# Second layer's weight conversion in a fused attention and two-layer kernel: in-place sums, four staging buffers, an earlier raw fetch

## The chip, the core and the metric

The kernel runs on one core of a Trainium2 chip. Its time is the device time of one execution in microseconds. Five engines work side by side, each with a queue of its own that it takes in order: TensorE (PE), VectorE (DVE), ScalarE (ACT), GpSimd (POOL) and SyncE (SP), which here issues all transfers between HBM and on-chip memory.

## What is computed

Attention through a small set of packed queries, then two feed-forward layers over 4608 tokens of width 512. The weights come as 64-bit floats.

```
p_packed = softmax(p @ k.T * scale) @ v          # 32 packed rows a head
x  = softmax(q @ p_packed.T * scale) @ p_packed   # 8 batches x 576 tokens, 8 heads x 64
h  = x @ w_in                                     # 512 -> 2048
x1 = (max(h, 0) + alpha * min(h, 0)) @ w_out      # 2048 -> 512
g  = x1 @ w_gate;  v = x1 @ w_val                 # 512 -> 1536
out = (g * sigmoid(g) * v) @ w_out2               # 1536 -> 512
```

## The kernel before

Matrix products are made of three products each, of a value rounded to a shorter format (hi) and its remainder (lo): hi by hi, hi by lo, lo by hi.

**First layer.** 256 iterations, each a group of 288 tokens by 128 hidden units. In iteration `it`, PE runs `h_unit(it)` (six matmuls into one of two PSUM banks "h"), then `o_unit(it - 3)` (twelve matmuls into four accumulators; `LAG1` is 3). Between them stands a chain over three engines: ACT makes `m` from h (L1003), DVE makes `g` from h and m (L1006) and so frees the bank, ACT rounds g to `hi` (L1014), POOL takes the difference `lo` (L1016). Attention of the later batches runs in between, by a table of half iterations: iteration `it` has the half `2*it`, ahead of `h_unit`, and `2*it + 1`, behind it. From iteration 224 on, the second layer's first tokens are made ready too: `split_x` rounds sums of x into ring tiles (L1120 on ACT, L1121 on DVE). Two of the eight ring tiles, tag D, take over the two buffers that the weight conversion works in.

**Conversion of the second layer's weights.** From half iteration 84 on. The 1536 hidden units are 12 blocks of 128 (`f`, 0 to 11). A block needs three raw pieces, of w_gate, w_val and w_out2, each 128 x 512 64-bit numbers. `widen` turns a piece into 32-bit floats by integer steps: SP fetches it into `raw` (L217); ACT takes the high words into a half tile `g` or `v` (L222); five steps follow on DVE (L224, L228, L237, L246, L254) and an addition on POOL (L265). From w_gate's and w_val's halves b11, b21, b12, b22 come four differences t1 to t4 (L927, POOL), since the second layer uses seven products in place of eight. Each of seven 256-column operands is split into hi (L933, ACT) and lo (L934, POOL) in a staging buffer and stored to HBM (L935, SP). w_out2's piece goes through `g` again and is split in 512 columns (L944, L945, L947). The tile `cva` with the lower number holds `raw`, `g` and `v`; the other one `t` and two staging buffers `st`, used in turn.

**What sets the order.** The conversion is a generator that yields "v" ahead of a DVE step and "p" ahead of a POOL or split step. `more_weights2` takes at most two steps in each half iteration, one "v" among them, and none of those in halves that attention keeps busy. The source order of all this is the wish only: the program is built by a scheduler that follows a simulated time line and lets instructions of one engine pass each other where their data allow it. After that the order on each engine is fixed, and the profile has exactly that order.

**Second layer.** Six groups of 768 tokens by 12 blocks, 72 steps of `gv_step`: seven products of six matmuls each (`product`), with ACT's p (L1204) and s (L1209) behind the first and the third, and the products with w_out2 of earlier steps between. The third product of a step (A12) reads x in the second ring tile and, in its second half, in the first tile of tag D; the fourth and fifth need the second tile of tag D. PE's order is the same in both programs.

## Time and profile before

| | us |
|---|---|
| median of 3 runs (1701.35 to 1706.72) | 1701.75 |
| the profiled execution | 1702.91 |
| its span, first to last instruction | 1701.1 |
| PE busy | 1609.9 (95%) |
| DVE, ACT, POOL busy | 868.2, 683.0, 708.8 |
| first layer's last matmul, second layer's first | 859.3, 859.5 |

The busy time of PE is not its peak: matmuls overlap. A row of the timeline gives start, length, engine, source line, operation and in brackets the idle time of the engine before it with what ended it. The view of waits adds such idle times up by the line that waited and the line or transfer waited for. The granted clock is 1.00 for 2.4 GHz and 0.5 for 1.2 GHz.

### The profile page before, as it was taken

To read this page: it belongs to the slowest core of one execution; us is meant where nothing else is said; L and a number is where in the kernel's file an instruction comes from. 1 tells how busy PE (TensorE), PEld (TensorE's weight loads), DVE (VectorE), ACT (ScalarE), POOL (GpSimd) and SP (SyncE) were. 2 spreads that over 40 slices of the span, in tenths; PEclk is the share of its full clock that TensorE was granted. 3 is DMA by queue.
4 is the path that set the end of the run, shared out by engine and by line. 5 is a ranking of instruction groups with operands and counts; after the bars stand their busy time and mean duration, and the time that the engine had idled before them with its cause. 6 is when DMAs were issued, how large, how long until landed. Compare 5 with 4: busy or idle time off the path is not lost.

```text
span 1701.1 us, 28474 instructions
## 1 busy us (share of the span) xinstructions
PE 1609.9 (95%) x10708; PEld 1456.6 (86%) x10708; DVE 868.2 (51%) x1549; ACT 683.0 (40%) x1511; POOL 708.8 (42%) x752
## 2 busy tenths in 40 slices
PE   5688899999999989999899999999999999999997
PEld 3467798988888888889899999999999999999997
DVE  6999757565756656565533443443443343244222
ACT  5774645555544555454522232232232232123122
POOL 3556744565554654547622322322322222232222
PEclk7799999999999999999999999999999999999999
DMA  9433464635445362644573463465455456445442
GB/s 238 121 102 115 120 159 115 165 95 155 130 108 143 117 156 53 150 138 139 182 274 141 177 237 139 166 202 185 164 211 182 158 191 202 159 174 185 156 173 81
DMA packets 227369, 266.11 MB, mean 156 GB/s; under 512 B 130464, under 2 KB 189856, under 8 KB 227232
## 3 DMA queue, kind: packets, MB, share of 16 engines
q1 hardware_dynamic: 227232, 264.30, 49.2%
q8 instruction: 84, 1.38, 0.3%
q14 instruction: 53, 0.43, 0.1%
HBM read 214.70 MB, written 49.55 MB: 155 GB/s over the span
## 4 chain that ended last, share of the span: by engine, by line
issue 39%; PE 25%; POOL 17%; DMA 7%; DVE 6%; ACT 4%; SPq 1%; POOLq 0%; ACTq 0%; DVEq 0%
POOL pl L1247 8%; PE acc L1029 5%; PE acc L1030 5%; PE acc L1035 5%; POOL s L1227 4%; DMA wgvd<-cva 4%; PE h L305 3%; PE h L307 2%; PE h L306 2%; POOL lo L1016 1%; DMA cva<-in_moe_w_gate_dram 1%; POOL cva L934 1%; DVE g L1006 1%; PE ppw L564 1%; POOL cva L265 1%
## 5 line engine op out<-in xcount | busy, mean ns | idle before, releaser
L1016 POOL TENSOR_TENSOR lo<-g,hi 128x288 fp32r<-128x288 f32 x256 | 227.5, 890 | 240.6 <-ACT hi L1014 187.8
L1227 POOL TENSOR_TENSOR s<-s,u 128x384 f32<-128x384 f32 x72 | 73.0, 1014 | 489.9 <-ACT s L1221 489.9
L1006 DVE SCALAR_TENSOR_TENSOR g<-h,sg,m 128x288 f32<-128x288 f32 x256 | 130.3, 509 | 162.2 <-ACT m L1003 132.0
L1184 DVE TENSOR_TENSOR u<-yb,p 128x384 f32<-128x384 f32 x144 | 80.1, 556 | 255.6 <-PE yb L307 255.6
L1247 POOL TENSOR_TENSOR pl<-s,ph 128x384 fp32r<-128x384 f32 x144 | 145.5, 1032 | 106.4 <-ACT ph L1245 106.4
L305 PE MATMUL h<-a2h,ppw 128*128 128x288 f32 x512 | 163.2, 319 | 27.0 <-DVE g L1006 21.4
L1184 DVE TENSOR_TENSOR u<-vb,u 128x384 f32<-128x384 f32 x144 | 80.4, 558 | 197.3 <-PE vb L307 196.9
L1014 ACT ACTIVATE hi<-g 128x288 fp32r<-128x288 f32 x256 | 113.1, 442 | 155.5 <-DVE g L1006 149.1
L307 PE MATMUL o<-wp,ph 128*128 128x512 f32 x432 | 171.5, 397 | 0.0
L306 PE MATMUL o<-wp,ph 128*128 128x512 f32 x432 | 170.9, 396 | 0.0
L305 PE MATMUL o<-wp,pl 128*128 128x512 f32 x432 | 168.8, 391 | 0.9 <-POOL pl L1247 0.9
L1221 ACT ACTIVATE s<-p 128x384 f32<-128x384 f32 x72 | 37.9, 526 | 302.0 <-DVE p L1184 302.0
L307 PE MATMUL h<-a2l,ppw 128*128 128x288 f32 x512 | 153.0, 299 | 0.0
L306 PE MATMUL h<-a2h,ppw 128*128 128x288 f32 x512 | 152.5, 298 | 0.0
L305 PEld LDWEIGHTS h<-a2h,ppw 128*128 128x128 f32 x512 | 97.9, 191 | 62.4 <-DVE g L1006 33.0
L305 PE MATMUL yb<-ring,gv 128*128 128x384 f32 x432 | 146.0, 338 | 0.2
L307 PE MATMUL yb<-ring,gv 128*128 128x384 f32 x432 | 144.4, 334 | 0.0
L306 PE MATMUL yb<-ring,gv 128*128 128x384 f32 x432 | 144.4, 334 | 0.0
L1003 ACT ACTIVATE m<-h,sal 128x288 f32<-128x288 f32 x256 | 125.6, 492 | 41.5 <-PE h L307 40.6
L1245 ACT ACTIVATE ph<-s 128x384 fp32r<-128x384 f32 x144 | 69.8, 519 | 121.3 <-DVE s L1225 121.3
L307 PEld LDWEIGHTS h<-a2l,ppw 128*128 128x128 f32 x512 | 98.0, 191 | 0.8 <-issue 0.8
L306 PEld LDWEIGHTS h<-a2h,ppw 128*128 128x128 f32 x512 | 98.4, 192 | 0.0
(232 smaller groups left out, 4187.1 us busy)
## 6 DMA issues: line engine op xcount, KB each, us to landing
gv<-wgvd SPq DMA_DIRECT2D x144, 896.0 KB, 6.2
wgvd<-cva SPq DMA_DIRECT2D x84, 256.0 KB, 2.6
cva<-in_moe_w_out_dram SPq DMA_DIRECT2D x28, 512.0 KB, 3.8
v<-in_v_dram SPq DMA_DIRECT2D x16, 576.0 KB, 5.4
out_dram<-os SPq DMA_DIRECT2D x12, 768.0 KB, 3.8
cva<-in_moe_w_in_dram SPq DMA_DIRECT2D x16, 512.0 KB, 3.9
kr<-in_k_dram SPq DMA_DIRECT2D x96, 72.0 KB, 2.8
qr<-in_q_dram SPq DMA_DIRECT2D x96, 72.0 KB, 2.5
```

Source lines behind the costliest of these rows:

```text
L305: nc.tensor.matmul(o, wlo, xhi, start=start, stop=False, **kw)
L306: nc.tensor.matmul(o, whi, xhi, start=False, stop=False, **kw)
L307: return nc.tensor.matmul(o, whi, xlo, start=False, stop=stop, **kw)
L1003: begun[it] = nc.scalar.activation(out=m, in_=hp, func=AF.Copy, scale=sal[:, f : f + 1])
L1006: made[it] = nc.vector.scalar_tensor_tensor(out=g32, in0=hp, scalar=sg[:, f : f + 1], in1=m, op0=ALU.mult, op1=ALU.max)
L1014: rounded[n] = nc.scalar.activation(out=hi, in_=x, func=AF.Copy)
L1016: nc.gpsimd.tensor_tensor(out=lo, in0=x, in1=f32(hi), op=ALU.subtract)
L1029: nc.tensor.matmul(acc[dc], lo[:, f % WP, c], ghi, start=start, stop=False)
L1030: last = nc.tensor.matmul(acc[dc], hi[:, f % WP, c], ghi, start=False, stop=False)
L1184: return nc.vector.tensor_tensor(out=out, in0=bank, in1=x, op=ALU.add)
L1227: latest.append(nc.gpsimd.tensor_tensor(out=s2, in0=s2, in1=u3, op=ALU.mult))
L1247: nc.gpsimd.tensor_tensor(out=lo, in0=x, in1=f32(hi), op=ALU.subtract)
```

## The change

Four things at once. The four sums are written over their sources (`less`), so the tile `t` is gone, and its room gives four staging buffers in place of two. The order of the splits follows: b11, b21 after w_gate's piece, b22 after w_val's, then four sums, then their four splits. w_out2's piece is split in two of 256 columns. The fetch is taken out of `widen`: `fetch2` issues the next raw piece as soon as `raw` has been read, and a new kind of step, "a", lets ACT's first step come only `LANDING` = 4 half iterations later. `more_weights2` may now take one "a", two "p" and one "v" in a half iteration, and three "v" from half iteration 448 on.

```
+LANDING = 4
+FREE0 = 448
     def widen(src, raw, val, out=None, n_piece=-1):
-        issued.append(nc.sync.dma_start(out=like(raw, src), in_=src))
+        if src is not None:
+            issued.append(nc.sync.dma_start(out=like(raw, src), in_=src))
...
-        spots["t"] = [b[:, i * 256 : (i + 1) * 256] for i in range(4)]
-        spots["st"] = [b[:, 1024 + i * 512 : 1536 + i * 512] for i in range(2)]
+        spots["st"] = [b[:, i * 512 : (i + 1) * 512] for i in range(4)]
...
+    def fetch2():
+        src = next(coming, None)
+        if src is not None:
+            nc.sync.dma_start(out=like(spots["raw"], src), in_=src)
+            spots["landed"] = spots["slot"] + LANDING
+
+    def piece2(name):
+        yield "a"
+        yield from widen(None, spots["raw"], spots[name])
+
+    def split2(full, out):
+        stage = spots["st"][spots["n"] % 4].bitcast(F32R)
+        spots["n"] += 1
+        hi, lo = stage[:, :256], stage[:, 256:]
         nc.scalar.activation(out=hi, in_=full, func=AF.Copy)
         nc.gpsimd.tensor_tensor(out=lo, in0=full, in1=f32(hi), op=ALU.subtract)
+        nc.sync.dma_start(out=out, in_=f32(stage).rearrange("p (t n) -> p t n", t=2))
...
+            yield from piece2("g")
+            yield "p"
+            fetch2()
+            split(0, b11)
+            yield "p"
+            split(2, b21)
+            yield from piece2("v")
+            yield "p"
+            fetch2()
+            split(6, b22)
+            for out, x, y in (b11, b12, b11), (b12, b22, b12), (b22, b22, b11), (b21, b21, b22):
+                yield "p"
+                less(out, x, y)
+            for k, full in (4, b11), (3, b12), (1, b22), (5, b21):
+                yield "p"
+                split(k, full)
+            yield from piece2("g")
+            for t in range(2):
+                yield "p"
+                if t == 0:
+                    fetch2()
+                c = slice(256 * t, 256 * t + 256)
+                split2(gv["g"][:, c], wo2d[f][:, :, c])
...
-    def more_weights2(vector):
+    def more_weights2(vector, slot):
-        for _ in range(2):
+        spots["slot"] = slot
+        left = dict(v=(3 if slot >= FREE0 else 1) if vector else 0, p=2, a=1)
+        while kinds[0] is not None and left[kinds[0]]:
+            if kinds[0] == "a" and slot < spots["landed"]:
+                return
```

The new program's line numbers are higher: L222 becomes L225, L265 L268, the subtraction L958, a split's hi L940 and lo L941; m is L1030, hi L1041, lo L1043, the ring split L1148, p L1232, s L1237. How the built order moves is shown at two places. The first is the end of block 2, on POOL, before:

```order
L265 TENSOR_TENSOR cva_101<-cva_101 128x512
L934 TENSOR_TENSOR cva_102<-cva_101,cva_102 128x256
L927 TENSOR_TENSOR cva_102<-cva_101 128x256 x2
L1016 TENSOR_TENSOR lo_4034<-g_82_4028,hi_4032 128x288
L927 TENSOR_TENSOR cva_102<-cva_101,cva_102 128x256 x2
L934 TENSOR_TENSOR cva_102<-cva_102 128x256
L1016 TENSOR_TENSOR lo_4077<-g_83_4071,hi_4075 128x288
L934 TENSOR_TENSOR cva_102<-cva_101,cva_102 128x256
L1016 TENSOR_TENSOR lo_4118<-g_84_4112,hi_4116 128x288
L934 TENSOR_TENSOR cva_102<-cva_102 128x256 x2
L1016 TENSOR_TENSOR lo_4184<-g_85_4178,hi_4182 128x288
L934 TENSOR_TENSOR cva_102<-cva_102 128x256
```

The same place on POOL after the change, iterations 93 to 95 (the last row is the lo of the fifth split):

```order
L268 TENSOR_TENSOR cva_101<-cva_101 128x512
L958 TENSOR_TENSOR cva_101<-cva_101 128x256 x2
L941 TENSOR_TENSOR cva_102<-cva_101,cva_102 128x256
L958 TENSOR_TENSOR cva_101<-cva_101 128x256
L1043 TENSOR_TENSOR lo_4477<-g_94_4471,hi_4475 128x288
L958 TENSOR_TENSOR cva_101<-cva_101 128x256
L941 TENSOR_TENSOR cva_102<-cva_101,cva_102 128x256 x3
L1043 TENSOR_TENSOR lo_4512<-g_95_4506,hi_4510 128x288
L941 TENSOR_TENSOR cva_102<-cva_101,cva_102 128x256
```

The nine small steps stand closer, with two lo of the first layer among them. On ACT at that place before, with the first step on w_out2's piece (L222) among the splits, which don't read what it writes:

```order
L933 ACTIVATE cva_102<-cva_102 128x256
L1014 ACTIVATE hi_4116<-g_84_4112 128x288
L933 ACTIVATE cva_102<-cva_101 128x256
L222 ACTIVATE cva_101<-cva_101 128x512
L933 ACTIVATE cva_102<-cva_102 128x256
L1003 ACTIVATE m_4179<-h_4171,sal 128x288
L933 ACTIVATE cva_102<-cva_102 128x256
L1014 ACTIVATE hi_4182<-g_85_4178 128x288
L1003 ACTIVATE m_4208<-h_4200,sal 128x288
L933 ACTIVATE cva_102<-cva_102 128x256
L1014 ACTIVATE hi_4211<-g_86_4207 128x288
L933 ACTIVATE cva_102<-cva_101 128x256
```

And after, where that step (L225) follows all five splits, whose lo have to be done before it:

```order
L940 ACTIVATE cva_102<-cva_101 128x256
L1030 ACTIVATE m_4472<-h_4464,sal 128x288
L1041 ACTIVATE hi_4475<-g_94_4471 128x288
L1030 ACTIVATE m_4507<-h_4499,sal 128x288
L940 ACTIVATE cva_102<-cva_101 128x256 x3
L1041 ACTIVATE hi_4510<-g_95_4506 128x288
L940 ACTIVATE cva_102<-cva_101 128x256
L1030 ACTIVATE m_4542<-h_4534,sal 128x288
L1041 ACTIVATE hi_4545<-g_96_4541 128x288
L225 ACTIVATE cva_101<-cva_101 128x512
```

The fifth split and the step on the next piece now stand one iteration apart. The second place is ACT at the change from the first layer to the second. Before, in iterations 250 and 251, the last conversion step (L944) and the splits of x into the first tile of tag D (`ring_10369`):

```order
L944 ACTIVATE cva_102<-cva_101 128x512
L1003 ACTIVATE m_10598<-h_10590,sal 128x288
L1014 ACTIVATE hi_10601<-g_251_10597 128x288
L1120 ACTIVATE ring_10369<-xr_03_9542 128x384
L1120 ACTIVATE ring_10369<-xr_10_9545 128x384
L1120 ACTIVATE ring_10369<-xr_11_9548 128x384
```

After, behind the last m and hi of the first layer, from p of the second layer's first step to its s (`ring_10393` and `ring_10443` are the tiles of tag D):

```order
L1232 ACTIVATE p_0_10813<-xb_10818 128x384
L940 ACTIVATE cva_102<-cva_101 128x256
L225 ACTIVATE cva_101<-cva_101 128x512
L940 ACTIVATE cva_102<-cva_101 128x256 x2
L1148 ACTIVATE ring_10393<-xr_03_9508 128x384
L1148 ACTIVATE ring_10393<-xr_10_9511 128x384
L1148 ACTIVATE ring_10393<-xr_11_9514 128x384
L1237 ACTIVATE s_0_10816<-xb_10818 128x384
```

The last block's conversion has moved from iteration 250 to behind the first layer's end, and the ring splits with it.

## Rows read from the trace of the kernel before

**Rows 1.** Busy time by stage: PE, weight loads, DVE, ACT, POOL; clock, DMA, GB/s

```profile
240.00:858.00 618.00, 586.09 (x5084) 534.73 (x5083) 367.94 (x659) 314.81 (x737) 343.27 (x389) 0.98 0.49 135
858.00:1700.00 842.00, 833.87 (x4333) 771.35 (x4331) 308.76 (x546) 218.97 (x456) 231.28 (x226) 1.00 0.49 177
```

**Rows 2.** Waits of PE, 240 to 858 us: total us, times, longest

```profile
PE h L305 <- DVE g L1006: 15.8, 16, 2.6
PE s L564 <- DVE kT L614: 4.2, 2, 3.2
PE et L678 <- ACT ppbd L702: 4.1, 4, 1.8
```

**Rows 3.** Waits of ACT in the same stretch

```profile
ACT cva L933 <- DMA wgvd<-cva: 47.9, 38, 3.5
...
ACT cva L222 <- DMA cva<-in_moe_w_val_dram: 22.4, 11, 3.7
ACT cva L222 <- DMA cva<-in_moe_w_gate_dram: 14.5, 7, 3.3
ACT cva L944 <- DMA wgvd<-cva: 11.2, 5, 4.7
ACT cva L933 <- POOL cva L927: 9.4, 7, 2.0
```

**Rows 4.** Timeline, 289 to 295 us, from a fetch to PE

```profile
289.26 0.38 SPq L217 DMA_DIRECT2D cva<-in_moe_w_val_dram  x1
...
292.57 0.66 ACT L222 ACTIVATE cva<-cva 128x512 f32<-128x512 f32 x1 [3.16 <-DMA cva<-in_moe_w_val_dram]
293.14 0.48 ACT L1003 ACTIVATE m<-h,sal 128x288 f32<-128x288 f32 x1
...
293.72 0.52 DVE L1006 SCALAR_TENSOR_TENSOR g<-h,sg,m 128x288 f32<-128x288 f32 x1
...
294.29 0.25 PEld L305 LDWEIGHTS h<-a2h,ppw 128*128 128x128 f32 x1 [2.86 <-DVE g L1006]
```

**Rows 5.** Busy time in a half-clock stretch and an undisturbed one

```profile
294.30:297.80 3.50, 3.50 (x15) 3.50 (x16) 3.50 (x9) 1.64 (x4) 0.80 (x1) 0.51 0.46 169
856.00:859.40 3.40, 3.40 (x28) 3.40 (x27) 0.01 (x1) 0.14 (x1) 0.52 (x1) 1.00 0.98 358
```

**Rows 6.** Timeline, the second layer's first step

```profile
860.76 0.49 ACT L1204 ACTIVATE p<-xb 128x384 f32<-128x384 f32 x1 [0.79 <-PE xb L307]
...
862.07 0.33 PE L305 MATMUL xb<-ring,gv 128*128 128x384 f32 x1
...
864.50 0.33 PE L307 MATMUL vb<-ring,gv 128*128 128x384 f32 x1
```

**Rows 7.** Groups by line and shape, 205 to 858 us: busy, mean ns, idle before

```profile
L1016 POOL TENSOR_TENSOR lo<-g,hi 128x288 fp32r<-128x288 f32 x221 | 195.1, 885 | 223.6 <-ACT hi L1014 172.2 <-PE acc L1035 35.1 <-PE h L307 9.1
...
L265 POOL TENSOR_TENSOR cva<-cva 128x512 f32<-128x512 f32 x36 | 47.5, 1318 | 16.5 <-DVE cva L254 12.3 <-ACT m L1003 2.1 <-PE ppt L626 2.1
...
L934 POOL TENSOR_TENSOR cva<-cva 128x256 fp32r<-128x256 f32 x48 | 38.1, 796 | 20.7 <-ACT cva L933 20.1 <-POOL lo L1016 0.4
...
L933 ACT ACTIVATE cva<-cva 128x256 fp32r<-128x256 f32 x84 | 34.5, 414 | 57.6 <-DMA wgvd<-cva 47.9 <-POOL cva L927 9.4
...
L237 DVE SCALAR_TENSOR_TENSOR cva<-cva 128x512 uint32<-128x512 uint32 x36 | 30.3, 841 | 0.4
...
L254 DVE SCALAR_TENSOR_TENSOR cva<-cva 128x512 f32<-128x512 uint32 x36 | 27.5, 764 | 0.6
...
L224 DVE TENSOR_SCALAR cva<-cva 128x512 f32<-128x512 f32 x36 | 16.9, 470 | 67.0 <-ACT cva L222 67.0
...
L1120 ACT ACTIVATE ring<-xr 128x384 fp32r<-128x384 f32 x12 | 5.8, 515 | 1.4 <-DVE xr L1111 0.7 <-DVE xr L1095 0.6
```

**Rows 8.** Transfers: KB each, median us from issue to landing

```profile
cva<-in_moe_w_gate_dram SPq DMA_DIRECT2D x12, 512.0 KB, 3.9
...
wo2d<-cva SPq DMA_DIRECT2D x24, 256.0 KB, 3.1
```

More of the change, by code (lines that the diff above doesn't have):

```diff
@@ L909, in weights2, with sources2 @@
         spots["g"], spots["v"] = a[:, 1024:1536], a[:, 1536:2048]
[L910 to L911 removed]
+        spots["st"] = [b[:, i * 512 : (i + 1) * 512] for i in range(4)]
         spots["n"] = 0
[L914 to L930 removed]
+    def sources2():
+        for f in range(NF2):
+            for w in w_gate, w_val:
+                yield w[:, 2 * f * P : 2 * (f + 1) * P].rearrange("(c p) f -> p c f", p=P)
+            yield w_out2[f * P : (f + 1) * P, :]
+    coming = sources2()
+    def fetch2():
[8 more added lines that the diff above has]
+        stage = spots["st"][spots["n"] % 4].bitcast(F32R)
         spots["n"] += 1
@@ L934, in product2 @@
         nc.gpsimd.tensor_tensor(out=lo, in0=full, in1=f32(hi), op=ALU.subtract)
-        nc.sync.dma_start(
-            out=wgvd[f][:, :, k, :], in_=f32(stage).rearrange("p (t n) -> p t n", t=2)
-        )
-    def rows2(f):
-        raw, val = spots["raw"], spots["g"]
-        yield from widen(w_out2[f * P : (f + 1) * P, :], raw, val)
-        yield "p"
-        stage = [t.bitcast(F32R) for t in spots["st"]]
-        nc.scalar.activation(out=stage[0], in_=f32(val), func=AF.Copy)
-        nc.gpsimd.tensor_tensor(out=stage[1], in0=f32(val), in1=f32(stage[0]), op=ALU.subtract)
-        for t in range(2):
-            nc.sync.dma_start(out=wo2d[f][:, t, :], in_=f32(stage[t]))
+        nc.sync.dma_start(out=out, in_=f32(stage).rearrange("p (t n) -> p t n", t=2))
@@ L949, in all_weights2, with split, less @@
     def all_weights2():
         weights2()
+        gv = {n: f32(spots[n]) for n in "gv"}
+        b11, b21 = gv["g"][:, :256], gv["g"][:, 256:]
+        b12, b22 = gv["v"][:, :256], gv["v"][:, 256:]
+        fetch2()
         for f in range(NF2):
-            yield from columns2(w_gate, "g", f)
-            yield from columns2(w_val, "v", f)
-            for i in range(len(PRODUCTS)):
-                yield from product2(f, i)
-            yield from rows2(f)
+            def split(k, full):
+                split2(full, wgvd[f][:, :, k, :])
+            def less(out, x, y):
+                nc.gpsimd.tensor_tensor(out=out, in0=x, in1=y, op=ALU.subtract)
+            yield from piece2("g")
[18 more added lines that the diff above has]
+                if t == 0:
+                    fetch2()
+                c = slice(256 * t, 256 * t + 256)
+                split2(gv["g"][:, c], wo2d[f][:, :, c])
@@ L959, in tile_kernel @@
     work2 = all_weights2()
     kinds = []
-    def more_weights2(vector):
-        for _ in range(2):
-            if not kinds:
-                kinds.append(next(work2, None))
-            if kinds[0] is None or kinds[0] == "v" and not vector:
+    def more_weights2(vector, slot):
+        spots["slot"] = slot
+        left = dict(v=(3 if slot >= FREE0 else 1) if vector else 0, p=2, a=1)
+        if not kinds:
+            kinds.append(next(work2, None))
+        while kinds[0] is not None and left[kinds[0]]:
+            if kinds[0] == "a" and slot < spots["landed"]:
@@ L968, in more_weights2 @@
                 return
-            vector = vector and kinds[0] == "p"
+            left[kinds[0]] -= 1
             kinds[:] = [next(work2, None)]
@@ L1299, in steps @@
             if slot >= GROUP0:
-                more_weights2(slot not in busy)
+                more_weights2(slot not in busy, slot)
     due = []
```

16 lines of the change are left out of this document (1 added, 15 removed).

## The prediction

> **What bounds the kernel now.** I read the busy time by stage first. In the second layer, from 858 us on, PE is busy for 833.87 of 842 us at full clock; between 240 and 858 us, where the first layer runs and the conversion beside it, PE is idle for 618 − 586.09 = 31.9 us and the granted clock has a mean of 0.98 [rows 1]. The half-speed share, 0.02 × 618, costs another 12.4 us. So 44 us is all that any change to the conversion can win here; the second layer has nothing to give, only to lose.
>
> Then the waits of PE in that stretch. The largest is h_unit's first matmul waiting for g (15.8 us), then the attention's transposes waiting for ACT's ppbd (4.1); 4.2 us wait for DVE's turned k, which the conversion hardly touches [rows 2]. What makes g and ppbd late stands in the waits of ACT: L933, the hi half of a split, waits 47.9 us for earlier stores of the staging buffers, L944, the same for w_out, 11.2, and L222, the first step on a raw piece, 22.4 and 14.5 us for its fetch [rows 3]. That is 59 us for stores and 37 for fetches, on an engine whose queue is in order, with m and hi of the first layer behind.
>
> How such a wait reaches PE is seen at one place: SP issues the fetch at 289.26, ACT stands idle for 3.16 us and starts L222 at 292.57; m comes at 293.14, g at 293.72, and PE's next weight load at 294.29, after 2.86 us of nothing [rows 4]. PE then runs at 0.51 of its clock for 3.5 us: 15 matmuls where 28 fit into 3.4 us at full clock [rows 5]. An ACT wait is not lost one for one, though. An undisturbed iteration is 18 matmuls that follow each other by 0.13 us (28 touch the 3.4 us from 856.0 on, two of them begun before [rows 5]), 2.38 us. There are two h banks, so h_unit of iteration i+2 needs g of i: two iterations less the six matmuls of h_unit (0.79) less m (0.48) and g (0.52) [rows 4] and their hand-offs leave about 2.9 us by which ACT may be late for nothing. Of 96 us of waits at ACT, PE pays at most 44.
>
> **The change: what goes.** With four staging buffers a split takes the buffer of the split four before it, in place of two, and in the order of the new program it stands many iterations behind that store; only the last of each block's group of five follows it by two iterations. I let the store waits go. Their part of the 44 us: by the waits at ACT 59 of 96, but the longest single waits are fetches, and of the 44 us PE's 4.2 for k with a share of the clock (6 us together) belongs to neither. I take half of 38, **19 us** gained; the ends are 10 (stores are many and short, so the slack hides them) and 23.
>
> **The fetch.** As written, ACT's L222 comes four half iterations, two iterations, after the fetch; before, both stood in the same half. But the order is made by a scheduler, and I counted there, for all 35 pieces after the first, how many iterations lie between DVE's last step on a piece (L254; POOL's add L265 and the next fetch follow it) and ACT's L222 on the next. Before: one four times, two 11, three 14, more six times. After: two 23 times, three five times, more seven times, never one. The scheduler had already put L222 two or three iterations behind. The need is L254's 0.8 us, the add's 1.32 [rows 7] and 3.9 us from issue to landing [rows 8], 6.0 us, and two iterations are 4.8. So the typical fetch still makes ACT wait 1 to 2 us, under the 2.9 us of slack; what goes are waits of over 3 us like that in [rows 4]. Of 19 us I take **9 us** gained, ends 0 (nothing moved) and 17.
>
> The trace shows fetches waited for with ACT's work right behind. The Trainium skill, in "DMA: Bandwidth & Descriptors", section "Rules for kernel authors", advises to issue a DMA early, compute, and wait on it late, so that its fixed cost is overlapped. By that rule the change as written would win all 19 us of this term and the sum below would be 10 us better; the counted order, in which the distance hardly grows, speaks against its being met here.
>
> **What is added on POOL.** The sums now overwrite their sources, so each split of a sum waits on ACT for its subtraction on POOL, and the first step on w_out's piece (L222, writing g) waits for the last split's lo, which reads g. Before, w_out's piece could overwrite g, whose last readers were early. In block 2 the new order has behind each other on POOL the add, four subtractions and five lo with two lo of the first layer: 1.32 + 9 × 0.80 + 2 × 0.885 = 10.3 us [rows 7], a subtraction priced as a lo of its shape. Counted from m of iteration 93: m, g and L254 take to about 1.9 us, POOL's lo of 93 to 2.5, and the last lo ends at 12.8. ACT, left alone, would come to L222 after three iterations (7.1 us), an m, a hi and their hand-offs, at 9 to 10.7 with the five hi. So it waits 2 to 3.5 us, and with L222's 0.66 and what follows m is late by about the slack or 1.5 us more. In blocks 0, 2, 5 and 7 the order leaves three iterations like this, in seven others four to six, where the slack covers the wait unless attention's steps fill ACT at that moment; the last block belongs to the next term. I take 1.2 us for each of the four and 0.45 for the seven, **8 us** lost; ends 0 and 24 (2 a block, half clock after some). Else the work is the same: 36 fetches, 108 stores as before, 48 subtractions; twelve 512-column splits become two of 256 columns, less than one L933 (0.41) more of ACT each [rows 7], which ACT's idle half hides [rows 1]; PE would pay it only where ACT is already 2.9 us late. The k and q loads queued behind on SP wait for the same adds and lo halves as before.
>
> **The change of stage.** This is the new loss that I am surest of. Before, ACT's last conversion step stands in iteration 250, and the three splits of x into the ring tile that takes over the raw piece's buffer (L1120) in iteration 251. After, the last block is still at work when the second layer starts: on ACT, p of the first step comes first, then the last split of the sums, L222 on the last w_out piece, its two splits, and only then those ring splits. PE needs them for the second half of its third product, which begins at 862.07 [rows 6]. p starts at 860.76 and takes 0.49 [rows 6], to 861.25. From there in a row: hi 0.41, lo 0.80, L222 0.66, five DVE steps of 0.47 to 0.84 (3.3 with the two not shown, which lie between), the add 1.32, two hi 0.83, the second lo's end 1.2 after them, a ring split 0.52 [rows 4, 7]: 9.0 us, 0.4 more for hand-offs, so PE goes on at 870.6, 8.5 us late. The next ring tile takes the staging buffers and waits for the last store, 3.1 us [rows 8] after the last lo; through it the fifth product ends some 10.5 us later than its last matmul's 864.50 [rows 6]. A hole as long leaves the clock at half for at least the 3.5 us of [rows 5], 1.7 us lost. Together **12.5 us** lost; ends 8 (PE catches the second wait up) and 17 (half clock for twice as long and more).
>
> **The sum.** −19 − 9 + 8 + 12.5 = −7.5 us. The profiled execution took 1702.9 us, 1701.1 of it the span; the change touches the span alone, so it would take 1695.4. The median of the runs lies 1.2 us under it, and rounding for hand-offs I have not counted leaves **1695 us** against 1701.75. A measurement of this kernel can tell a change from none at about 0.3%, 5.1 us.
>
> **The rivals.** First, that the change does what it says: the fetch is there in time, the full 17 is won, stores 21, POOL's groups cost 3 and the change of stage 11. −24, 1678 us. For it speaks that no piece is left at a distance of one iteration; against it the counts above. Chance 0.12.
>
> Second, the gain is given back whole: stores give 12, fetches 6, POOL's groups cost 6 and the change of stage 12.5: 0, 1702 us. For it speaks that a wait taken from ACT is worth nothing where it lay within the slack; 38 store waits of 47.9 us are 1.3 us each [rows 3]. Chance 0.27.
>
> Third, slower: POOL becomes the bound of each block's end. If ACT is late there by 1.7 us more than PE forgives, 12 × 1.7 = 20 us are lost; with stores at 15, fetches at 4 and 13 for the change of stage, +14, 1716 us. It decides from 19 + 9 − 12.5 = 15.5 us, 1.3 us a block. Against it speaks that only in four blocks does ACT come as early as in the one worked out; for it, that one hole of 3 us costs 1.7 more of clock [rows 5]. Chance 0.22.
>
> **How the numbers follow.** The forecast has 0.39, spread over 1688 to 1702, so that 0.29 of it counts as faster and 0.10 as the same. Faster: 0.29 + 0.12 = 0.41; the same: 0.10 + 0.27 = 0.37; slower 0.22. The range leaves out the first rival's better half and the third's worse half: 1680 to 1716.
>
> **What would show it.** In the changed kernel's waits, L933's for stores should fall below 15 us and ACT's first step should wait for fetches for 25 to 45 us; waits of L933 for POOL's subtractions, 9.4 us now in the same list, and of L222 for POOL should have grown to 20 us or more. PE should stand still for 7 to 10 us in the first step of the second layer, with half clock behind. PE's idle time up to that point should be 15 to 28 us in place of 31.9. If there is no hole at the start of the second layer, the term of 12.5 is wrong; if fetch waits are under 10 us, the counted order misled me; if PE's idle time before 840 us has not fallen, the third rival has it.

## The result, and the profile of the changed kernel

The changed kernel takes **1676.22 us** (median; 1675.40 to 1677.72) against 1701.55 before (four runs): a ratio of **0.984**, interval 0.982 to 0.986. It is faster by 25 us, where I had said 7 and a range that ended at 1680. Timed once more on another chip (E12) its ratio was 0.982, 0.980 to 0.985.

The profiled execution has a span of 1674.7 us, 26.4 less than before. Where they come from is read from one event, the first matmul of the second layer (xb): it begins at 820.64 us in place of 859.46, so the first layer won 38.8 us. From there to the end it is 854.1 us in place of 841.6, so the change of stage lost 12.5. Busy time by stage (stretch, its length, then PE, weight loads, DVE, ACT, POOL, each with its instructions; granted clock, DMA share, GB/s), to be held beside [rows 1]:

```profile
240.00:820.00 580.00, 572.69 (x5102) 527.40 (x5100) 356.79 (x652) 316.70 (x738) 330.76 (x394) 1.00 0.52 142
820.00:823.40 3.40, 3.40 (x19) 3.08 (x19) 1.20 (x3) 1.51 (x4) 2.73 (x4) 1.00 0.96 302
823.40:834.00 10.60, 0.01 (x1) 0.00 (x0) 2.85 (x7) 2.36 (x6) 3.40 (x4) 0.60 0.89 343
834.00:839.20 5.20, 5.19 (x16) 4.89 (x17) 3.95 (x8) 2.63 (x6) 0.00 (x0) 0.50 0.82 249
840.00:1674.00 834.00, 825.99 (x4286) 763.92 (x4285) 306.27 (x541) 217.21 (x452) 231.32 (x226) 1.00 0.49 174
```

In the first layer PE is now idle for 580 − 572.69 = 7.3 us where it was 31.9, and the clock is whole but for one short stretch. Then comes a hole of 10.6 us in which PE does nothing, and 5.2 us behind it at half clock, the level of 1.2 GHz. Beside [rows 2], the waits of PE from 240 to 860 us (total, times, longest):

```profile
PE xb L308 <- ACT ring L1148: 10.6, 1, 10.6
PE h L308 <- DVE g L1033: 5.7, 6, 2.3
PE s L567 <- DVE kT L617: 1.6, 3, 1.2
```

h_unit's waits for g fell from 15.8 us to 5.7; the one wait of 10.6 is new. Beside [rows 3], the waits of ACT's conversion steps, 240 to 820 us (L225 is L222 of before, L940 is L933):

```profile
ACT cva L225 <- DMA cva<-in_moe_w_gate_dram: 15.9, 10, 2.5
ACT cva L940 <- POOL cva L268: 15.2, 23, 2.1
ACT cva L225 <- DMA cva<-in_moe_w_val_dram: 14.1, 10, 3.1
...
ACT cva L225 <- POOL cva L941: 6.9, 6, 1.7
ACT cva L940 <- POOL cva L958: 6.7, 12, 1.2
...
ACT cva L940 <- POOL lo L1043: 4.0, 2, 2.0
ACT cva L940 <- DMA wgvd<-cva: 3.4, 3, 1.6
```

Before, in the list of [rows 3], there are also these:

```profile
ACT cva L222 <- POOL cva L934: 3.3, 3, 1.9
ACT cva L222 <- DMA cva<-in_moe_w_out_dram: 3.2, 2, 2.0
ACT cva L222 <- POOL cva L945: 2.5, 1, 2.5
ACT cva L944 <- POOL cva L265: 2.0, 4, 1.1
...
ACT cva L222 <- POOL cva L927: 0.9, 1, 0.9
```

The waits for stores went from 59 us to 3.4. Those for fetches went from 40 (the prediction's 37 leave out the 3.2 for w_out's pieces) only to 30, as the counted order had said. All waits of the conversion steps for POOL's adds, sums and lo grew from 18 to 33. What they cost PE can't be read from this list.

### The profile page after: what moved, and what is told of

Same layout as the page of the kernel before. It is cut to its first block, busy times and chain, and to the rows that moved or that the text cites. A ratio compares the mean times of both kernels' runs of the same rounds, so it can differ in the third digit from the quotient of the medians.

```text
span 1674.7 us, 28539 instructions
## 1 busy us (share of the span) xinstructions
PE 1607.0 (96%) x10708; PEld 1456.6 (87%) x10708; DVE 860.1 (51%) x1549; ACT 689.7 (41%) x1523; POOL 702.9 (42%) x764
## 4 chain that ended last, share of the span: by engine, by line
issue 36%; POOL 13%; PE 1%; DMA 0%; POOLq 0%; ACT 0%; DVE 0%; ACTq 0%; DVEq 0%
POOL pl L1275 9%; POOL s L1255 4%; POOL xr L1116 0%; DMA out_dram<-os 0%; POOLq L1275 0%; PE yb L310 0%; PE yb L308 0%; PE yb L309 0%; PE vb L310 0%; PE vb L309 0%; PE vb L308 0%; PE o L308 0%; PE o L310 0%; POOL cva L941 0%; PE o L309 0%
## 5 line engine op out<-in xcount | busy, mean ns | idle before, releaser
L1043 POOL TENSOR_TENSOR lo<-g,hi 128x288 fp32r<-128x288 f32 x256 | 224.5, 877 | 251.6 <-ACT hi L1041 180.4
L1041 ACT ACTIVATE hi<-g 128x288 fp32r<-128x288 f32 x256 | 113.0, 442 | 138.0 <-DVE g L1033 133.4
L1030 ACT ACTIVATE m<-h,sal 128x288 f32<-128x288 f32 x256 | 126.1, 493 | 61.4 <-PE h L310 60.1
L308 PEld LDWEIGHTS h<-a2h,ppw 128*128 128x128 f32 x512 | 98.1, 192 | 47.6 <-DVE g L1033 18.8
L308 PE MATMUL xb<-ring,gv 128*128 128x384 f32 x288 | 96.6, 335 | 10.6 <-ACT ring L1148 10.6
```

The lines of the kernel that those rows point to most:

```text
L308: nc.tensor.matmul(o, wlo, xhi, start=start, stop=False, **kw)
L1030: begun[it] = nc.scalar.activation(out=m, in_=hp, func=AF.Copy, scale=sal[:, f : f + 1])
L1041: rounded[n] = nc.scalar.activation(out=hi, in_=x, func=AF.Copy)
L1043: nc.gpsimd.tensor_tensor(out=lo, in0=x, in1=f32(hi), op=ALU.subtract)
```

## The experiments

The lines of a kernel's steps shift with its edit; the tile names (cva for the conversion's buffers) stay. Every run was timed in rounds beside the kernel before on its own chip, whose median there lay between 1704 and 1710. Two numbers from each trace say more than the time. One is where the second layer's first matmul begins, which keeps the two stages apart. The other is the time from the g of iteration 68 to that of 255, by which the run is shorter than before's 557.7 us: it leaves out the start and the change of stage. The last column sums the rows of ACT's conversion steps waiting for stores and for fetches, from 205 us to the first layer's end (the kernel before waits for fetches for 43 us from 205 us on, for 40 from 240 us on).

| run | median us | ratio (interval) | second layer from | its length | g 68 to 255 | stores + fetches |
|---|---|---|---|---|---|---|
| before | 1701.55 | | 859.5 | 841.6 | 0 | 59 + 43 |
| changed | 1676.22 | 0.984 (0.982 to 0.986) | 820.6 | 854.1 | −35.3 | 3 + 30 |
| E1 | 1680.09 | 0.984 (0.981 to 0.988) | 831.6 | 842.1 | −25.8 | 0 + 38 |
| E2 | 1696.04 | 0.994 (0.992 to 0.996) | 833.0 | 863.4 | −24.3 | 32 + 38 |
| E3 | 1674.57 | 0.981 (0.978 to 0.984) | 834.2 | 840.7 | −29.4 | 0 + 35 |
| E4 | 1684.04 | 0.986 (0.983 to 0.990) | 843.1 | 840.8 | −16.8 | 5 + 35 |
| E5 | 1675.95 | 0.982 (0.980 to 0.984) | 830.3 | 847.5 | −24.4 | 5 + 39 |
| E6 | 1688.85 | 0.990 (0.986 to 0.993) | 839.7 | 843.9 | −18.8 | 37 + 36 |
| E7 | 1697.49 | 0.994 (0.993 to 0.996) | 824.5 | 870.8 | −30.7 | 2 + 26 |
| E8 | 1673.64 | 0.980 (0.979 to 0.982) | 830.6 | 841.1 | −25.6 | 5 + 35 |
| E9 | 1670.30 | 0.978 (0.976 to 0.980) | 826.0 | 845.1 | −30.4 | 8 + 32 |
| E10 | 1705.87 | 0.999 (0.997 to 1.000) | 862.3 | 842.3 | +0.7 | 58 + 40 |
| E11 | 1683.00 | 0.985 (0.983 to 0.987) | 840.1 | 841.7 | −22.3 | 27 + 41 |
| E12 | 1678.95 | 0.982 (0.980 to 0.985) | 824.1 | 855.6 | −31.7 | 8 + 34 |
| E13 | 1714.34 | 1.003 (1.001 to 1.004) | 865.5 | 842.6 | +3.2 | 27 + 82 |
| E14 | 1722.75 | 1.008 (1.006 to 1.010) | 829.2 | 892.7 | −29.5 | 33 + 27 |
| E15 | 1667.75 | 0.975 (0.972 to 0.977) | 821.8 | 845.7 | −34.6 | 8 + 31 |
| E16 | 1716.67 | 1.007 (1.004 to 1.009) | 873.3 | 841.7 | −31.2 | 0 + 54 |
| E17 | 1671.95 | 0.981 (0.977 to 0.984) | 830.7 | 840.3 | −34.1 | 48 + 2 |
| E18 | 1703.71 | 0.999 (0.997 to 1.001) | 857.7 | 842.5 | −42.0 | 0 + 0 |

The stage columns are of one execution each; the changed kernel's two (820.6 and E12's 824.1) differ by 3.5 us, so smaller differences are not read. The four runs of E1 spread over 9 us and those of E6 over 11, and E1's profiled run is its fastest, 4.6 us under its median; what is read between two single traces is rough by as much.

### The change taken apart, from the changed kernel's side

**E1, the buffers alone.** The changed kernel with before's fetch and pace (shown is the fetch; the calls of `fetch2` go too, and `more_weights2` is as before):

```
-    def piece2(name):
-        yield "a"
-        yield from widen(None, spots["raw"], spots[name])
+    def piece2(name):
+        yield from widen(next(coming), spots["raw"], spots[name])
```

> The changed kernel with the fetch as before (issued in the same half iteration as ACT's first step on the piece, in program order) and the pace of before; what is left of the change is the sums in place and the four staging buffers. Against 1701.6 before and 1676.2 after. Theory A, stores: the waits for stores are worth far more than the 19 us that I gave them, since they come several in a row before one m and the lateness adds up over iterations; four buffers alone win 32 to 40 us of the first layer, 1662 to 1670, and ACT's waits for stores fall under 10 us while those for fetches stay above 35. Theory B, fetch: the distance of four half iterations is what does it; buffers alone give 1690 to 1702. Theory C, both halves are needed, each worth about half: 1680 to 1688. By my own prediction (19 for stores less 8 for POOL): 1690. The last conversion step falls in iteration 253 here, so 0 to 3 us of a hole at the second layer's start may be in it.

**E2, two buffers.** `spots["st"][spots["n"] % 4]` becomes `% 2`.

> The changed kernel with two staging buffers in place of four; fetch, pace, sums in place as changed. Theory A, stores: nearly all of the first layer's gain of some 38 us goes, 1705 to 1716, with ACT waiting for stores over 45 us again. Theory B, fetch: 1676 to 1684. Theory C, each half: 1690 to 1698. By my prediction's sizes (19 back): 1695. The hole of 10.6 us at the second layer's start stays in all of them, since the conversion ends no earlier.

**E3, no distance.** `LANDING = 4` becomes `LANDING = 0`.

> The changed kernel with the distance of four half iterations set to zero: the fetch is still issued as soon as the raw buffer is free, but ACT's first step on the piece isn't held back. It ends the conversion in iteration 238, so the hole at the second layer's start (10.6 us and half clock behind it) should be gone in any case, worth 11 to 13 us: 1664 if the distance is worth nothing (theory A). If the distance is what won the first layer's time (theory B), ACT's waits for fetches rise from 30 to 45 us or more and the first layer loses 10 to 20 us again: 1674 to 1684.

**E6, neither.** E1 with `% 2`: sums in place and the new order of the splits are all that is left of the change.

> The kernel of E1 with two staging buffers in place of four: sums in place, the splits in the new order (two of g ahead of v's piece), fetch and pace of before. Neither part that the change names is left. If the buffers and the distance are the whole gain, the first layer ends where it does before, 856 to 860 us, and the time is 1698 to 1704. If the new order of the splits alone, which puts them further apart, takes a part of the store waits, 840 to 850 us and 1682 to 1694, with ACT's waits for stores at 25 to 40 us in place of 59.

In E1 and E3 the first layer gives back 11 and 13.6 us of its 38.8, in E2 12.4. E6 is the surprise: with neither of the two parts that the change names, 19.8 us are won. So of 38.8 us some 20 come from the order of the splits, some 8 from four buffers on top (E6 to E1), some 11 from the distance and its pace on top of both (E1 to the changed kernel), 7.5 by E12. The last two sizes are no larger than the spread of E1 and E6. Theory C was nearest, but none of the three had the order in it, and E2's time owes 9 us to its hole at the change of stage, which I had expected to stay and which grew to 18.8 us. E3 shows the other side of the distance: without it the conversion ends in iteration 238, there is no hole, and the time is that of the changed kernel. In the time as a whole the distance brought nothing here.

What the distance takes away in the first layer is not fetch waits in the main: E3 has 35 us of them and the changed kernel 30. It is waits of ACT for POOL. In E3, 205 to 834 us (the lines are those of the changed kernel):

```profile
ACT cva L940 <- POOL cva L268: 25.8, 30, 2.4
...
ACT cva L940 <- POOL cva L958: 16.4, 36, 1.0
...
ACT cva L225 <- POOL cva L941: 14.5, 12, 1.7
```

These are 57 us, 50 in E1, and 31 in the changed kernel. That PE's loss comes by them is a reading of the lists; no run changes them alone.

### The order

**E10, w_out in halves,** and **E11, the new order**, each put alone into the kernel before; E11's core:

```
             yield from columns2(w_gate, "g", f)
+            yield from product2(f, 0)
+            yield from product2(f, 2)
             yield from columns2(w_val, "v", f)
-            for i in range(len(PRODUCTS)):
+            for i in (6, 4, 3, 1, 5):
                 yield from product2(f, i)
```

(the four subtractions move behind the split of b22).

> The kernel before with one thing of the change: w_out's piece is split in two halves of 256 columns, each in its own staging buffer with one store, in place of one of 512 columns over both buffers with two stores. E6 won 20 us of the first layer with neither four buffers nor the distance. If the 512-column split is what costs (it waits for both buffers, 11.2 us in five waits before, and the next block's first split waits for both stores), 8 to 14 us come back: first layer 845 to 852, 1688 to 1694 against 1701.6. If it is the order of the other splits, under 3 us: 1699 to 1703.

> The kernel before with one thing of the change: the order of a block, two splits of g ahead of v's piece, v's own right behind it, then the four subtractions and the other four splits. Sums still go to their own buffers, two staging buffers, w_out as before. If the order is what won E6's 20 us (splits further apart find their buffer's store done), 12 to 20 us: first layer 840 to 848, 1683 to 1690, with ACT's waits for stores down from 59 to 35 to 45 us. If the sums in place or w_out's halves won it, under 4 us: 1698 to 1703.

E10 gave nothing that can be told from before, E11 the whole of E6's gain: 19.4 us, with two buffers, the sums in their own place and the old fetch. ACT's waits in E11, 205 to 840 us:

```profile
ACT cva L929 <- DMA wgvd<-cva: 26.8, 21, 3.3
ACT cva L222 <- DMA cva<-in_moe_w_val_dram: 21.3, 12, 2.6
ACT cva L222 <- DMA cva<-in_moe_w_gate_dram: 18.6, 10, 2.9
```

Seven splits in a row on two buffers each wait for a store; two ahead of v's piece and five behind it wait half as long.

### The two terms by themselves, in the old order

**E13, four buffers,** the sums in the raw buffer to make room:

```
-        spots["t"] = [b[:, i * 256 : (i + 1) * 256] for i in range(4)]
-        spots["st"] = [b[:, 1024 + i * 512 : 1536 + i * 512] for i in range(2)]
+        spots["t"] = [a[:, i * 256 : (i + 1) * 256] for i in range(4)]
+        spots["st"] = [b[:, i * 512 : (i + 1) * 512] for i in range(4)]
```

> The kernel before, its order of a block kept (four subtractions, then seven splits in a row), with four staging buffers; the room comes from putting the four sums into the raw piece's buffer, which is free between v's piece and w_out's. This is my term of 19 us for the stores, taken alone. If the new order won its 20 us because splits that stand apart find their store done (store waits reach PE), four buffers take the same waits away here: ACT's store waits under 15 us, first layer 832 to 842 in place of 859.5. If the order won by spreading the seven splits' work over more iterations, buffers give only what they gave on top of it, 8 us (E6 to E1): 848 to 855, although the store waits are gone. The conversion ends in iteration 255, so a hole of 3 to 8 us may follow in the second layer: 1680 to 1690 by the first, 1696 to 1705 by the second.

E13 settled nothing by itself, since it traded one wait for another. ACT's waits, 205 to 866 us:

```profile
ACT cva L222 <- DMA cva<-in_moe_w_out_dram: 33.0, 12, 4.7
...
ACT cva L933 <- DMA wgvd<-cva: 26.7, 24, 2.9
ACT cva L222 <- DMA cva<-in_moe_w_val_dram: 25.3, 12, 3.7
ACT cva L222 <- DMA cva<-in_moe_w_gate_dram: 23.6, 11, 3.5
```

The stores' 59 us fell to 27, but w_out's fetch now waits for the sums in its buffer, 33 us, and the others wait longer: 109 us in all in place of 102, and 3 us lost. What ACT waited for had changed, how long hardly, and PE's time neither. Four buffers in the old order have so not been tried without another wait in their place.

**E14, the distance alone,** with the changed kernel's fetch2, piece2 and pace in the kernel before:

```
-            yield from columns2(w_gate, "g", f)
-            yield from columns2(w_val, "v", f)
+            yield from piece2("g")
+            yield "p"
+            fetch2()
+            yield from piece2("v")
+            yield "p"
+            fetch2()
```

> The kernel before, its order of a block, sums and two staging buffers kept, with the fetch issued as soon as the raw buffer is free and ACT's first step on the piece at least four half iterations later, and the changed kernel's pace. This is my term of 9 us for the fetch, taken alone. On top of the new order the distance won 7 us with two buffers (E6 to E2) and 10 to 14 with four (E3 to the changed kernel). If it adds to the order: first layer 846 to 853. If it needs the new order or the four buffers: 855 to 860. If, by holding the pieces apart, it does what the order does: 838 to 846. The end of the conversion lies in the second layer as in the changed kernel, so 10 to 20 us of a hole come on top: 1700 to 1716.

The first layer won 30 us, more than any of the three expectations (at most 21). But part of it is work put off: by the g of iteration 236 ACT has begun 29 of the 36 pieces, 31 in the changed kernel and 33 before; four of E14's begin only in the second layer, and PE pays there, 46 us where I had expected 10 to 20 (waits of PE from 820 us on):

```profile
PE xb L308 <- ACT ring L1146: 46.1, 1, 46.1
```

**E16, no waits for stores:** the store reads a weight tile of the first layer, `wout[3][0]`, in place of the staging buffer. **E17, no waits for fetches:** from the first block's w_out on the fetch goes to a DRAM tensor. **E18:** both. The cores (the stores of w_out's piece are changed alike, and a hint that each store be issued after its lo is not shown):

```
-            out=wgvd[f][:, :, k, :], in_=f32(stage).rearrange("p (t n) -> p t n", t=2)
+            out=wgvd[f][:, :, k, :],
+            in_=f32(wout[3][0][:, 0, :]).rearrange("p (t n) -> p t n", t=2),
...
-        issued.append(nc.sync.dma_start(out=like(raw, src), in_=src))
+        if spots.get("n", 0):
+            issued.append(nc.sync.dma_start(out=like(rawd, src), in_=src))
+        else:
+            issued.append(nc.sync.dma_start(out=like(raw, src), in_=src))
```

> The kernel before, but every store of a split reads a weight tile of the first layer in place of the staging buffer, so no split waits for a store; number, size and moment of the stores (after the lo) stay. It leaves out that the converted weights reach the second layer. This is the store term alone, in the old order, where I said 19 us (10 to 23): first layer 840 (836 to 850) in place of 859.5. If the waits for stores are what the new order took away (E11, 840.1), 836 to 844. If the order won by spreading the splits and not by the waits, 852 to 860.

> The kernel before, but from the second block on each fetch lands in a scratch tensor in DRAM, so that ACT's first step on a piece waits for no fetch, only for the steps on the piece before it; it leaves out the weights of the second layer from there on. The fetch term alone, in the old order, with stores as before: I said at most 17 to 19 us for all fetch waits, 9 for what the change takes: first layer 841 to 850. If the distance wins by holding the pieces apart (E14 won 30 us of the first layer with 32 us of fetch waits left), the waits themselves are worth little: 852 to 860.

> E16 and E17 together: no waits for stores, and none for fetches from the second block on. If the terms add as I did it, 19 + 17: first layer 823 to 832. If the two waits stand in for one another (what is taken from one turns up as the other, as in E13), each alone gives little and both together give 25 to 36 us. If density is what costs and not the waits, 845 to 858, far above the changed kernel's 820.6, although it has no DMA wait left and the changed kernel has 36 us of them.

E16 and E18 are slower than they should be for a reason that I built in. A store that reads a finished tile is tied to nothing, and all 108 were issued by 303.25 us, not after their lo as I had expected and the hint had asked. SP in E16 (start, time, engine, line, times in a row):

```profile
269.43 5.83 SPq L936 DMA_DIRECT2D wgvd<-wo3h  x7
...
277.19 4.87 SPq L936 DMA_DIRECT2D wgvd<-wo3h  x6
...
284.28 4.27 SPq L936 DMA_DIRECT2D wgvd<-wo3h  x5
```

x1p and v, which the first layer needs, stood behind them, and PE waited (205 to 320 us):

```profile
PE acc L1034 <- DVE x1p L1052: 26.6, 2, 25.7
PE pp L694 <- DMA v<-in_v_dram: 11.4, 1, 11.4
```

From iteration 68 on (297 us before, 341 in E16 and 337 in E18) this is over, which is why the sixth column begins there. In that stretch E16 wins 31 us, E17 34 and both together 42. E16 and E18 have no stores there at all, so the transfers are gone with the waits: the DMA share is 0.49 before, 0.38 in E16 and 0.28 in E18. E11 and the changed kernel, with all transfers in place, win 22 and 35. ACT's waits in E17, 205 to 831 us, show that most of the stores' were left, 48 us of 59:

```profile
ACT cva L937 <- DMA wgvd<-cva: 43.3, 41, 3.2
...
ACT cva L948 <- DMA wgvd<-cva: 4.3, 3, 1.9
...
ACT cva L227 <- DMA cva<-in_moe_w_val_dram: 2.1, 1, 2.1
```

Either wait alone, taken away, is worth three quarters of both or more: 31 + 34 is not 42. In these runs and those with two buffers, the sixth column held against the seventh shows the same. From 102 us of DMA waits to 68 to 73 (E11, E6, E2) 19 to 24 us are won, from there to 50 to 59 (E14, E16, E17) 30 to 34, and the last 50 bring only 8 more (E18). It is no rule for all runs: E1 has 38 us of DMA waits left and wins 26, E17 has 50 and wins 34.

What is missing in that column is POOL. With ACT's waits for POOL added, all in the stretch of the sixth column, most runs fall into line: 105 us of waits before, 91 in E6 for 19 us won, 75 to 81 in E1, E2, E3 and E11 for 22 to 29, 64 to 70 in E9, E12, E14 and E16 for 30 to 32, 58 to 59 in E7, E15, E17 and the changed kernel for 31 to 35, 22.5 in E18 for 42. Only E4, E5 and E8 (below) win less than their sums of 66 to 75 would say, 17 to 26. So it seems to matter how long ACT waits in all, and little what for; that is a count over the traces and not an experiment. How late ACT's m comes shows the same: of the 186 iterations from 70 on it begins over 2 us after h_unit's last matmul in 54 before, in 43 in E11, in 18 in the changed kernel.

### POOL, and the end of the conversion

**E7, every lo twice,** in split2:

```
         nc.gpsimd.tensor_tensor(out=lo, in0=full, in1=f32(hi), op=ALU.subtract)
+        nc.gpsimd.tensor_tensor(out=lo, in0=full, in1=f32(hi), op=ALU.subtract)
```

> The changed kernel with every split's lo computed twice on POOL, the same subtraction into the same place: 108 more POOL instructions of 0.8 us, 86 us of POOL's time, up to seven of them (5.6 us) in a block's group. My prediction put 8 us on POOL's groups as they are, by the rule that ACT's L225 waits for the last lo of the group and m is then late. If POOL's chain is at that limit, each of the 12 blocks loses 2 to 4 us and half clock after some: first layer 845 to 870 us, 1700 to 1725. If it has slack, as the 7.7 us that L225 waits for POOL's lo in seven times suggest, the first layer ends at 820 to 828 us, and only the hole at the second layer's start grows by 1 to 3 us (the last block's lo are in its chain): 1677 to 1686.

POOL is busy for 394 us in the stretch in which it was for 331 (240 to 820 us):

```profile
240.00:820.00 580.00, 569.16 (x5074) 523.78 (x5073) 353.82 (x645) 312.55 (x731) 394.33 (x483) 1.00 0.50 136
```

The second layer still begins at 824.5 us, E12's place. POOL has slack in the first layer: ACT waits 40 us for it, 34 in the changed kernel, and so much less for fetches, 26 us in place of 30. Only the hole behind the first layer grew, from 10.6 to 25.9 us, where I had expected 1 to 3 us more.

**E4, E5, E8, an earlier end:** `FREE0` 320 with three DVE steps in a half iteration; 384 with two; 384 with three.

> The changed kernel with the faster pace of the last blocks (three DVE steps in a half iteration) from half iteration 320 on in place of 448. The conversion ends in iteration 241. If the hole of 10.6 us in the second layer's first step is the late conversion, it goes with its half clock: 11 to 13 us less than 1676.2, 1663 to 1666, below both kernels. Rival: the same steps pushed together on DVE delay g and cost the first layer 5 to 12 us of it: 1668 to 1676. If the hole has another cause (the ring's own sums), it stays and so does 1676.

> The changed kernel, but from half iteration 384 on two DVE steps in a half iteration (the changed kernel: three, from 448 on). The last conversion step stands in iteration 254, the ring tile's first split in 255, so the hole in the second layer (12.5 us) should go or shrink to 1 or 2 us. E4, three steps from 320 on, lost 22 us of the first layer against the changed kernel, 0.24 us an iteration. If that loss comes from the three DVE steps in a row, two cost little: first layer ends at 820 to 825 us, 1662 to 1668 in all. If it comes from the conversion being denser at all (one piece following the last more closely on every engine), the 62 iterations from 384 on cost 5 to 10 us: 1668 to 1675.

> As E5, with three DVE steps from half iteration 384 on. Last conversion step in iteration 251, the ring's splits at the places of the kernel before, so no hole. By E4's loss of 0.24 us an iteration over 62 iterations: first layer 828 to 836 us, 1670 to 1678. If E4's loss belonged to its own places alone (blocks 7 to 9): 821 to 826, 1662 to 1668.

The hole goes as it should (E8: 841.1 us for the second layer; in E5 PE waits 3.4 us for a load of gv in its place). But all three lose in the first layer as soon as the denser pace begins: E4 22 us, E5 and E8 10 (19 and 6 against E12). E4's 1684 us lies above both expectations. PE in E4, until its pace changes and after, is busy for 317.87 of 320 and 201.54 of 220 us, in the changed kernel for 318.59 and 215.15:

```profile
240.00:560.00 320.00, 317.87 (x2916) 289.40 (x2915) 201.08 (x374) 175.54 (x407) 177.19 (x211) 1.00 0.50 132
560.00:780.00 220.00, 201.54 (x1734) 182.57 (x1733) 138.26 (x246) 114.57 (x276) 135.31 (x160) 0.97 0.56 159
```

Two steps cost as much as three, so it is not the DVE steps in a row; E4's DMA waits (40 us) are hardly longer than E1's (38). That denser pieces cost is shown, by which engine is not.

**E9, raw and staging tiles last in the ring; E15, the same at an even pace; E12, the changed kernel again.**

```
-X_RING = "AADDAAAA"
+X_RING = "AAAAAADD"
```

and for E15 also `FREE0 = 999`.

> The changed kernel with the ring of the second layer's x taking over the raw and staging tiles last, as seventh and eighth of its tiles in place of third and fourth, so that nothing of the first step waits for the conversion; conversion and pace as changed. If the hole of 10.6 us is that takeover and nothing else, the first layer ends at 820 to 822 us, the second takes 841 to 843: 1662 to 1666 us, below both kernels, and without E8's loss of 10 us for a denser end. Rival: the four further weight tiles that the ring now takes come free late as well, and PE waits 3 to 8 us for them instead: 1666 to 1673.

> The changed kernel itself once more, beside E9 on the same chip: 1674 to 1680 us by either theory, first layer to 820 us, hole of 10 to 11 us. If its first layer ends over 828 us here, the 11 us between it and E1 and E3 are within what one execution differs from another, and no statement on the distance stands on them.

> E9 (raw and staging tiles last in the ring) without the faster pace at the end: one DVE step in a half iteration throughout. E9 lost some 5 us with half clock in three places behind half iteration 448 and 4 us in the second layer's first step, where the last block's steps stand ahead of p. If the dense end costs the first, 2 to 5 us less in the first layer; but more of the last block falls behind the layer's change. 1665 to 1669 if that is hidden, 1670 to 1678 if it costs PE as much again.

E9 beats both kernels, 1670.3 us against E12's 1678.95 beside it. E15 has the lowest time of all, 1667.75, a ratio of 0.975; its interval overlaps with E9's, so only its lead on the changed kernel is certain. Busy time of E15 up to the change of stage and over it:

```profile
240.00:820.00 580.00, 573.65 (x5099) 528.56 (x5098) 355.36 (x655) 317.87 (x741) 331.50 (x389) 0.99 0.51 139
820.00:840.00 20.00, 17.69 (x94) 16.79 (x93) 7.95 (x15) 7.11 (x16) 11.00 (x14) 0.91 1.03 394
```

PE is idle for 2.3 us of the 20 after 820, where the changed kernel had a hole of 10.6, and a clock of 0.91 costs 1.8 more: the 4 us by which the second layer is longer than before. The last block's steps still run there beside it.

## Why the prediction was wrong

**What bounds the kernel: right.** 44 us was all that the conversion could win; without any DMA wait (E18) 42 were won, with the change 35 in the same stretch.

**How ACT's waits would change: right for the stores and fetches, not for POOL.** Store waits under 15 us (3.4) and fetch waits of 25 to 45 (30) came, and so did the hole, 10.6 us in place of 7 to 10. Waits for POOL's subtractions and of L225 for POOL should have come to 20 us and are 14 (6.7, 6.9 and 0.6); the largest new wait is that of the splits for POOL's add, 15.2, which the forecast does not name. And PE's idle time up to the hole, forecast at 15 to 28 us, is 7.3. That sign points at the step that failed.

**What they are worth: this is the step that failed.** I shared the 44 us out by ACT's waits, took half of 38 for the stores and half of what was left for the fetches. For the first layer the terms −19 − 9 + 8 come to −20; the trace has −38.8, E12's −35.4. Of the 19 us between, 8 are the POOL term below, the rest the worth of the waits. Two things were wrong in it. The terms are not shares: each alone is worth 31 to 34 us of 42, as E16 and E17 show. The reason that I see is that PE pays only for what exceeds the 2.9 us that it forgives, and that either wait, taken away, takes most of what exceeds it. The traces fit that: by how much m begins later than 2.9 us after h_unit's last matmul adds up, over the 186 iterations from 70 on, to 22.5 us before, 3.6 in E16, 4.0 in E17 and 0.7 in E18. No run changed the slack itself, so it stays argued. And I took the stores below their share of the waits (59 of 96, 23 us), with the reason that the longest single waits are fetches, which is misread: [rows 3] have a store wait of 4.7 us, and 3.7 is the longest for a fetch. The stores' waits, 1.3 us each in L933, came seven splits in a row, and E11, which only puts the splits apart, won 19.4 us.

**The fetch.** That the distance hardly grows was counted rightly, and fetch waits fell by little. That it would therefore win little was wrong for the first layer: on top of the rest it won some 11 us there (E1 to the changed kernel), alone up to 30 (E14). The prediction looked at the fetch alone; what fell with the distance was above all ACT's waits for POOL (E3, 57 us to 31). The Trainium skill, "DMA: Bandwidth & Descriptors", section "Rules for kernel authors", advises to issue a DMA early and wait on it late; by it I had the sum 10 us better and set it aside. E17, 34 us better with fetches that are not waited for, bears out that such waits are worth taking away. The change as written did not take them away: 30 us of fetch waits are left.

**POOL, +8: wrong.** More work in POOL's groups cost the first layer nothing that can be told; with twice the lo (E7) the second layer begins 0.4 us later than in E12. I had added up the chain of one block in which ACT comes early, and let m be late by all of it; L225's waits for POOL are there (6.9 us), 1.7 us at the longest, under the 2.9 of slack.

**The change of stage, +12.5: right,** 854.1 − 841.6 = 12.5, in E12 14.0. ACT at that place (start, time, line, what it does, idle before and its releaser):

```profile
821.94 0.49 ACT L1232 ACTIVATE p<-xb 128x384 f32<-128x384 f32 x1 [0.26 <-PE xb L310]
825.33 0.42 ACT L940 ACTIVATE cva<-cva 128x256 fp32r<-128x256 f32 x1 [2.89 <-DMA wgvd<-cva]
826.58 0.66 ACT L225 ACTIVATE cva<-cva 128x512 f32<-128x512 f32 x1 [0.83 <-POOL cva L941]
831.51 0.72 ACT L940 ACTIVATE cva<-cva 128x256 fp32r<-128x256 f32 x2 [4.28 <-POOL cva L268]
833.44 1.35 ACT L1148 ACTIVATE ring<-xr 128x384 fp32r<-128x384 f32 x3 [1.21 <-POOL cva L941]
```

It is the chain of the prediction, step for step, with one wait more: 2.89 us of L940 for a store. So the first hole was 10.6 us in place of 8.5, half clock cost 2.6 us behind it (half of 5.2) in place of 1.7, and the second hole, of two us, didn't come. The mechanism was right; that the sum is exact is luck.

**The rivals.** The time came out at the first one's, 1678, to which I gave 0.12. Its terms (17 and 21 won, 3 and 11 lost) were nearer than mine because it gave the waits their whole worth. It too was right by luck in part: it let the fetches be there in time, and ACT still waits 30 us for them. Against it I had put the counts of the distance, and they were no evidence against the stores.

## What to carry to other kernels

Where an engine has slack in every iteration, don't share a loss out over its causes by their length: ask what each removal alone leaves above the slack, and expect the first to bring most and the last little. Splitting a run of short waits into two runs can bring most of what removing them brings (22 us in E11, 31 in E16, in the same stretch); try the order before the memory. And when work is stretched out, look at who takes over its buffers at the end: here some 9 us of PE were lost to the order of eight ring tiles.

## What was not expected of the hardware

The clock follows such holes closely. In the changed kernel PE stands still from 823.4 us; the clock is at half from 825.5 until 839.2, so 5.2 us of work ran at half speed behind 10.6 of nothing. In E14, with a hole of 46 us, it was at half for 47.8 us, in E7, with 26, for 23.9, most of it in the hole itself and 5.7 and 3.3 us behind it. In E1 the longest wait of PE, 2.4 us, left no half-clock stretch, and none of the others did; in the first layer of the kernel before there are seven such stretches from 205 us on, 27 us together, behind waits of 1.2 to 3.2 us. At half clock 27 us cost 13.6: half of the 27.9 us that E1's first layer won. Why one wait of some 2.5 us brings such a stretch and another doesn't is open.
